# A hidden layer in two equal passes: one and a half chunks each instead of one and two

## The chip, the cores and the metric

The kernel runs on one core of a Trainium2 chip. The metric is the device time of one execution in microseconds, the median of the runs shown; the profile is of one further execution.

## The reference

`x` is 8 x 4224 x 192 in float32. First a causal convolution: each of 8 heads (24 channels) has 7 taps, normalized by a softmax. Then a feed-forward block with a residual, without biases:

```python
w = np.exp(w - max(w)); w = w / (sum(w) + 1e-09)
out = np.einsum('hk,bskhg->bshg', w, x_unf)       # x_unf: 7 shifted views of x
xn = (x - mu) / np.sqrt(var + 1e-06) * g_ln       # x is now out
ch = np.maximum(xn @ w_ch1, 0.0) @ w_ch2          # 192 -> 768 -> 192
return x + ch
```

## The kernel before

Tokens are worked off in 18 groups; a full group has 16 tokens in each of 128 partitions. The convolution of group g + 1 runs on VectorE (`conv`, six taps for each of 8 heads, one `scalar_tensor_tensor` each) while TensorE works on group g. The first two taps come from ScalarE (`first_tap`, `second_tap`) and are added by DMA on POOL's queue. VectorE also transposes y in 32 x 32 blocks to `yt`, so that channels lie on partitions in strips of 32.

Groups 3 to 17 are *mixed*: both matmuls are done as a 2 x 2 Strassen-Winograd product with seven products instead of eight. In the first matmul (`up_mixed`) the token halves and channel halves of `yt`, their sums (`ysums`), the quarters of the first weight and their sums (`w1sums`) enter; the quarters of the result are c11, c12, c21 and c22 of the hidden tile `room`. In float32 a matmul leaves two pairs of LDWEIGHTS and MATMUL records, and the four 32-row strips of TensorE run together.

A quarter has FC = 3 chunks of 128 hidden channels and 8 x 32 = 256 columns of tokens for each strip. PSUM has two sets of four banks of 512 columns, X and Y, one bank a strip. The seven products are therefore made in two passes: pass `one` with a single chunk (256 columns of a bank), then pass `two` with two chunks (512 columns). Products alternate between X and Y, so a product needs that the set of the product before the last was read. Each product is followed by one of:

- `evict`: ScalarE copies the set to a quarter (line L642);
- `close` with a part: ScalarE copies it to a part (L642), and a DMA on POOL's queue adds the part to a quarter (L609);
- `close` without one: VectorE adds the set to the quarter (L648).

Finished quarters get a relu in place on ScalarE (L655); c21 gets `lower_sum` on VectorE (L811), which also applies its relu and subtracts c11 for the second matmul. Then `down_fast` (L835) does the second matmul with seven products of its own on six banks, the first of which are those of X and Y; ScalarE copies them (L841), and between its products ScalarE does the rest of the relus, the scaling of the group before (L914) and the first taps of a later group.

There is no scheduler: each engine works off its instructions in the order of the program text, and an instruction that waits holds up those behind it on its engine. So the place of every call in `up_mixed` matters. In pass two the order around the change is: after the second product an eviction with its DMA; after the third and fourth an eviction each, with the relu of pass one's c11 (`one.relu(one.c11)`) behind the third; then on VectorE taps 2 to 4 of all heads and tap 5 of four heads (28 instructions, L417), the fifth product's close by DMA, the sixth product, the relu of pass two's c11, then on VectorE `lower_sum` of pass one, three more instructions of tap 5, and `close(c21)`; then the seventh product and its eviction.

`next(ahead)` stands for the last sums and transposes of the group before on VectorE (`finish_fast`), `next(pending)` for the halves of a reciprocal square root on POOL. `work` is the list of ScalarE's pieces that `down_fast` places between its products. In the last group the closes of pass two are on VectorE, `lower_sum` of pass one stands behind `close(c21)`, and four of the 16 tokens are left to a plain matmul at the end (`keep`, `down_row`).

Of the kernel before, what the change touches and what calls it, by code (L numbers as in the profile page):

```python
# [16 lines left out]
def kernel(  # L17
# [34 lines left out]
    P = 128  # L52
# [440 lines left out]
    def hidden_tile(g):  # L493
        n = groups[g][2]

        if fast[g]:
            ht[g] = room.rearrange(
                "p (h e f q j t) -> p h e f q j t", h=2, e=2, f=FC, q=NQ, t=width(g)
            )
        else:  # L500
            ht[g] = room[:, 0 : NF * NQ * n * C].rearrange(
                "p (f j q t) -> p f j q t", f=NF, q=NQ, t=C
            )
# [104 lines left out]
    def add_by_dma(dst, src):  # L608
        nc.gpsimd.dma_start(out=dst, in_=src, accum_op=ALU.add)  # L609

    def up_mixed(g, ahead, pending):


        W = HJ * C
        last = g + 1 == NG
        assert groups[g][2] == 2 * HJ and PAIR * W == 512 and FC == PAIR + 1
# [3 lines left out]
        s1, s2, s3, s4 = ysums[g]  # L620
        done = groups[g - 1][2]

        class Pass:
            def __init__(self, f0, f1, chain, other):
                self.n, self.chain, self.other = f1 - f0, chain, other
                self.b11, self.b12, self.b21, self.b22 = quarters_of_w1(f0, f1)
                self.t = [v[:, :, P * f0 : P * f1] for v in (w1sums[:, k] for k in range(3))]
                (self.c11, self.c12), (self.c21, self.c22) = [
                    [a[:, h, e, f0:f1].rearrange("p f q j t -> p f q (j t)") for e in range(2)]
                    for h in range(2)  # L630
                ]

            def product(self, to, left, right, first=True, end=True):
                rows_of_tiles(to, left, right, first, end, True)

            def seen(self, banks, f=None):
                src = banks[:, :, 0 : self.n * W] if f is None else banks[:, :, W * f : W * f + W]
                return src.rearrange("p q (f w) -> p f q w", w=W)

            def evict(self, banks, dst, relu=False, f=None):  # L640
                src = self.seen(banks, f)
                nc.scalar.activation(dst, src, AF.Relu) if relu else nc.scalar.copy(dst, src)  # L642

            def close(self, c, banks, part=None, f=None):


                if part is None:
                    nc.vector.tensor_tensor(c, c, self.seen(banks), op=ALU.add)  # L648
                    return
                self.evict(banks, part, f=f)  # L650
                whole = "p f q w -> p (f q w)"
                add_by_dma(c.rearrange(whole), part.rearrange(whole))

            def relu(self, c):
                nc.scalar.activation(c, c, AF.Relu)  # L655

        def parts(pool, tag):

            room = pool.tile([P, J * D], F32, tag=tag, name=f"parts_{tag}{g}")
            return room.rearrange("p (f q w) -> p f q w", q=NQ, w=W)  # L660

# [10 lines left out]
        one, two = Pass(PAIR, FC, X, Y), Pass(0, PAIR, Y, X)  # L672
        p = one
        p.product(X, a11, p.b11, True, False)
        p.evict(X, p.c11)
        p.product(Y, a12, p.b21)
        p.close(p.c11, Y, two.c12[:, 0:1])
        next(pending, None)
        p.product(X, s2, p.t[0], False, False)
        p.evict(X, p.c21)  # L680
        p.product(Y, s3, p.t[1], True, False)
        p.evict(Y, p.c22)
        p.product(X, s1, p.b12, False, False)
        p.close(p.c22, X, two.c12[:, 1:2])
        next(pending, None)
        p.product(Y, a22, p.t[2], False)
        p.close(p.c21, Y, two.c22[:, 0:1])
        p.product(X, s4, p.b22, False)
        p.evict(X, p.c12, True)

        next(ahead)
        p = two
        rooms = parts(cpool, "cs"), parts(bpool, "tb")
        p.product(Y, a11, p.b11, True, False)
        p.evict(Y, p.c11)
        p.product(X, a12, p.b21)
        if last:
            p.close(p.c11, X)
        else:
            for f in range(PAIR):  # L700
                p.close(p.c11[:, f : f + 1], X, rooms[0][:, f : f + 1], f)
            if g == 3:
                store_y(g, nc.gpsimd)
        act_scales(0, 1)
# [8 lines left out]
        p.product(Y, s2, p.t[0], False, False)  # L713
        p.evict(Y, p.c21)
        one.relu(one.c11)
        p.product(X, s3, p.t[1], True, False)
        p.evict(X, p.c22)
        act_scales(1, 2)
        p.product(Y, s1, p.b12, False, False)
        taps_of_next(2, 5)  # L720
        taps_of_next(5, 6, heads=(0, H // 2))
        p.close(p.c22, Y, None if last else rooms[1][:, 0:PAIR])
        p.product(X, a22, p.t[2], False)
        for f in range(PAIR):
            p.relu(p.c11[:, f : f + 1])
        if last:
            one.relu(one.c22)
        else:
            lower_sum(g, (PAIR,))
            taps_of_next(5, 6, heads=(H // 2, H - 1))  # L730
        p.close(p.c21, X)
        if last:
            lower_sum(g, (PAIR,))
        p.product(Y, s4, p.b22, False)
# [3 lines left out]
        lower_sum(g, range(PAIR))  # L738
        if last:

            n = J - fast[g]
            kept = xpool.tile([P, J + PAD, D], F32, tag="xg", name=f"kept{g}")
            kept = kept.rearrange("p j d -> p (j d)")[:, 0 : NF * n * P]
            kept = kept.rearrange("p (f j q h t) -> p f j q h t", f=NF, q=NQ, h=2, t=T)
            rows_left[g] = kept.rearrange("p f j q h t -> p f j (q h t)")

            def keep(f, h):
                src = a[:, h, f // FC, f % FC, :, fast[g] :].rearrange("p q j t -> p j q t")
                nc.scalar.activation(kept[:, f, :, :, h], src, AF.Relu)

            keeping = [lambda f=f, h=h: keep(f, h) for f in range(NF) for h in range(2)]
# [13 lines left out]
        work += [lambda j=j: scale_one(j) for j in range(2, done)]  # L765
        half = [lambda i=i: two.relu(two.c22[:, i : i + 1]) for i in range(PAIR)]
# [29 lines left out]
    def of_products(g):  # L796
        return ht[g][:, :, :, :, :, 0 : fast[g] * T // width(g), :]

    def half_sum(g, dst, left, right, op, fs=range(FC)):
        a = of_products(g)  # L800
        for f in fs:
            nc.vector.tensor_tensor(  # L802
                a[:, *dst, f], a[:, *left, f], a[:, *right, f], op=op
            )

    def lower_sum(g, fs=range(FC)):

        a = of_products(g)
        if g in MIXED:
            for f in fs:  # L810
                nc.vector.scalar_tensor_tensor(  # L811
                    out=a[:, 1, 0, f], in0=a[:, 1, 0, f], scalar=0.0, in1=a[:, 0, 0, f],
                    op0=ALU.max, op1=ALU.subtract,
                )
        else:
            half_sum(g, (1, 0), (1, 0), (0, 0), ALU.subtract, fs)

    def down_fast(g, work):
# [3 lines left out]
        a = of_products(g)  # L822
# [3 lines left out]
        free = a[:, 1, 0].rearrange("p f q j t -> p (f q) j t")  # L826
        parts = [free[:, 0:CH], free[:, CH : 2 * CH]]
        banks = [take_bank() for c in range(CH) for i in range(2)]

        def product(bank, left, right, to, first, behind=0):  # L830
            for c in range(CH):
                dst = banks[2 * c + bank]
                for f in (PAIR, *range(PAIR)):
                    for q in range(NQ):
                        nc.tensor.matmul(  # L835
                            dst[C * q : C * q + C, 0:w], right[:, f, C * c : C * c + C],
                            left[:, f, q], start=(first and f == PAIR), stop=(f == PAIR - 1),
                            skip_group_check=True,
                        )
                if to is not None:  # L840
                    nc.scalar.copy(  # L841
                        to[:, c], dst[:, 0:w].rearrange("p (j t) -> p j t", t=t)
                    )
                for one in work[:behind]:
                    one()
                del work[:behind]
# [15 lines left out]
        product(0, a[:, 0, 0], b[0], c11, True, behind[0])  # L862
        product(1, a[:, 1, 0], w2sums[:, 2], c22, True, behind[1])
        product(1, a[:, 1, 1], w2sums[:, 3], c21, False, behind[2])
        product(1, a[:, 0, 1], b[2], None, True, behind[3])
# [8 lines left out]
        for c in range(CH):  # L874
            nc.vector.tensor_tensor(
                c11[:, c], c11[:, c], banks[2 * c + 1][:, 0:w].rearrange("p (j t) -> p j t", t=t),
                op=ALU.add,
            )
        product(0, a[:, 1, 1], w2sums[:, 1], parts[0], False, 2)
        product(0, a[:, 0, 0], w2sums[:, 0], parts[1], False, 2)  # L880
        for one in work:
            one()
        product(0, a[:, 0, 1], b[3], c12, False)
# [207 lines left out]
```

## Time and profile before

| | |
|---|---|
| time, median of 3 runs | 956.37 us (956.06 to 957.61) |
| the profiled execution | 959.62 us |
| its span in the profile | 957.5 us |
| TensorE matmul busy | 950.6 us (99%) |
| VectorE busy | 890.7 us (93%) |
| ScalarE busy | 696.6 us (73%) |
| POOL busy | 338.4 us (35%) |
| L533, share of the chain that ended last | 47% |
| L835, share of the chain that ended last | 44% |
| one first matmul of a mixed group, 504 records | 27.96 us |
| one second matmul of a mixed group, 504 records | 27.44 us |

PE is TensorE's matmuls, PEld its weight loads, DVE VectorE, ACT ScalarE, POOL GpSimd. "In the records" means the start times of single instructions in the trace. The granted clock of TensorE was 1.00 in every stage looked at. The profiled execution's time is more than its span by what lies around the program.

### The profile page before, as it was taken

The page shows a single profiled execution, that of the slowest core. Times are in us where ns is not written, and L with a number is a line of the kernel's source. Part 1 is how long each engine was busy: PE and PEld are TensorE (multiplying, and loading weights), DVE is VectorE, ACT ScalarE, POOL GpSimd, SP SyncE. Part 2 cuts the span into 40 slices and gives each one's busy share as a digit, 9 for nine tenths or more (in the row PEclk, how much of TensorE's full clock was granted, in tenths as well). Part 3 has the DMA queues.
Part 4 walks back from the last instruction along what each step waited for, and adds up shares of the span by engine and source line. Part 5 has one row for each costly group of instructions (what it writes and reads, how often), then busy time and mean ns, then how long its engine had stood idle before and what let it go on. Part 6 is the DMA issues. An engine that isn't in the chain of part 4 may idle for free.

```text
span 957.5 us, 37878 instructions
## 1 busy us (share of the span) xinstructions
PE 950.6 (99%) x16858; PEld 743.1 (78%) x16858; DVE 890.7 (93%) x1489; ACT 696.6 (73%) x1165; POOL 338.4 (35%) x472
## 2 busy tenths in 40 slices
PE   9999999999999999999999999999999999999998
PEld 8998896876869697787968778695867769586787
DVE  7999999999999998999999999999999999999757
ACT  6853678596877959687795968779695877967462
POOL 1058422623145141533227141452316232261310
PEclk9999999999999999999999999999999999999999
DMA  8359589689697988979697896969889696778251
GB/s 204 101 160 212 98 230 280 121 187 229 135 263 138 249 156 181 224 132 277 127 249 151 196 220 127 278 131 252 155 197 205 124 276 132 175 136 138 42 96 68
DMA packets 39544, 168.82 MB, mean 176 GB/s; under 512 B 4437, under 2 KB 8150, under 8 KB 33367
## 3 DMA queue, kind: packets, MB, share of 16 engines
q0 software_dynamic: 32576, 106.25, 59.8%
q1 hardware_dynamic: 6800, 60.16, 17.3%
q8 instruction: 132, 2.16, 0.9%
q14 instruction: 30, 0.25, 0.1%
q10 hardware_dynamic: 6, 0.00, 0.0%
HBM read 38.93 MB, written 50.33 MB: 93 GB/s over the span
## 4 chain that ended last, share of the span: by engine, by line
PE 97%; POOL 1%; DMA 1%; ACT 0%; issue 0%; DVE 0%; ACTq 0%; POOLq 0%
PE ps L533 47%; PE ps L835 44%; PE ps L772 4%; PE ps L367 1%; DMA room<-room 1%; PE ps L326 1%; ACT room L642 0%; POOL room L609 0%; POOL d L460 0%; PE ps L354 0%; POOL r L483 0%; POOL d L479 0%; DVE yt L428 0%; POOL d L478 0%; PE ps L335 0%
## 5 line engine op out<-in xcount | busy, mean ns | idle before, releaser
L417 DVE SCALAR_TENSOR_TENSOR y<-xg,taps,y 128x384 f32<-128x384 f32 (+3 forms) x720 | 364.8, 583 | 1.9 <-DMA y<-room 1.3
L835 PE MATMUL ps<-room,w2sums 128*32 128x256 f32 (+2 forms) x4608 | 247.4, 371 | 0.0
L533 PE MATMUL ps<-yt,w 32*128 32x256 f32 (+2 forms) x4104 | 234.8, 378 | 0.3 <-DVE yt L428 0.3
L642 ACT COPY room<-ps 128x1024 f32<-128x1024 f32 (+1 forms) x135 | 175.0, 1296 | 78.6 <-PE ps L533 77.8
L533 PEld LDWEIGHTS ps<-yt,w 32*128 32x128 f32 x4104 | 204.1, 185 | 25.8 <-issue 8.7
L835 PEld LDWEIGHTS ps<-room,w2sums 128*32 128x32 f32 x4608 | 153.5, 110 | 87.8 <-ACT room L655 5.3
L835 PE MATMUL ps<-room,w 128*32 128x256 f32 (+2 forms) x3456 | 189.8, 371 | 0.1
L802 DVE TENSOR_TENSOR room<-room 128x1024 f32<-128x1024 f32 (+2 forms) x147 | 161.2, 1172 | 22.7 <-PE ps L835 16.1
L835 PEld LDWEIGHTS ps<-room,w 128*32 128x32 f32 x3456 | 113.9, 110 | 67.9 <-DVE room L648 5.0
L533 PE MATMUL ps<-ysums,w1sums 32*128 32x256 f32 x2160 | 125.3, 379 | 0.2 <-issue 0.2
L533 PEld LDWEIGHTS ps<-ysums,w1sums 32*128 32x128 f32 x2160 | 109.1, 185 | 11.2 <-ACT room L642 3.6
L925 POOL DMA_DIRECT2D out_dram<-ot x69 | 58.9, 940 | 159.3 <-ACT ot L914 102.6
L409 POOL DMA_DIRECT2D y<-tb x59 | 52.4, 1384 | 155.0 <-ACT room L841 110.2
L841 ACT COPY cs<-ps 128x256 f32<-128x256 f32 (+2 forms) x192 | 70.2, 367 | 45.6 <-PE ps L835 45.5
L655 ACT ACTIVATE room<-room 128x1024 f32<-128x1024 f32 (+1 forms) x89 | 92.5, 1072 | 0.8 <-DMA room<-parts_cs 0.8
L914 ACT ACTIVATE ot<-ot,r 128x192 f32<-128x192 f32 x224 | 90.9, 464 | 0.0
L380 ACT ACTIVATE y<-xg,taps 128x384 f32<-128x384 f32 (+3 forms) x141 | 73.1, 608 | 0.2 <-DMA xg<-in_x_dram 0.2
L448 DVE BATCH_NORM_STATS2 st<-y 128x6 f32<-128x192 f32 x264 | 70.1, 344 | 0.0
L841 ACT COPY room<-ps 128x256 f32<-128x256 f32 (+2 forms) x96 | 35.5, 369 | 46.5 <-PE ps L835 43.8
L398 ACT ACTIVATE tb<-xg,taps 128x384 f32<-128x384 f32 (+1 forms) x120 | 66.0, 627 | 0.0
L533 PE MATMUL ps<-yt,w1sums 32*128 32x256 f32 x1080 | 65.3, 380 | 0.4 <-ACT room L642 0.4
L533 PE MATMUL ps<-ysums,w 32*128 32x256 f32 x1080 | 64.6, 376 | 0.0
(113 smaller groups left out, 918.0 us busy)
## 6 DMA issues: line engine op xcount, KB each, us to landing
xg<-in_x_dram SPq DMA_DIRECT2D x14, 2112.0 KB, 16.6
room<-room POOLq DMA_DIRECT2D x45, 512.0 KB, 5.1
out_dram<-ot POOLq DMA_DIRECT2D x59, 384.0 KB, 9.6
y<-tb POOLq DMA_DIRECT2D x58, 384.0 KB, 8.5
out_dram<-y SPq DMA_DIRECT2D x13, 1536.0 KB, 9.5
room<-parts_cs POOLq DMA_DIRECT2D x28, 512.0 KB, 6.8
room<-parts_tb POOLq DMA_DIRECT2D x14, 1024.0 KB, 7.6
xg<-in_x_dram POOLq DMA_DIRECT2D x1, 2112.0 KB, 13.6
```

Source lines behind the costliest of these rows:

```text
L380: nc.scalar.mul(y[g][:, 0:n, cs], xg[g][:, 0:n, cs], taps[:, h, 0:1])
L398: nc.scalar.mul(tb[g][:, 0:n, cs], xg[g][:, 1 : 1 + n, cs], taps[:, h, 1:2])
L417: nc.vector.scalar_tensor_tensor(out=y[g][:, 0:n, cs], in0=t[:, k : k + n, cs], scalar=taps[:, h, k : k + 1], in1=y[g][:, 0:n, cs], op0=AL ...
L448: nc.vector.bn_stats(out=sums[g][:, j, :], in_=y[g][:, j, :])
L533: nc.tensor.matmul(banks[:, q, i * w : i * w + w], right[rows, c, P * i : P * i + P], left[rows, :, c, :], start=(first and c == 0 and i = ...
L642: nc.scalar.activation(dst, src, AF.Relu) if relu else nc.scalar.copy(dst, src)
L655: nc.scalar.activation(c, c, AF.Relu)
L802: nc.vector.tensor_tensor(a[:, *dst, f], a[:, *left, f], a[:, *right, f], op=op)
L835: nc.tensor.matmul(dst[C * q : C * q + C, 0:w], right[:, f, C * c : C * c + C], left[:, f, q], start=(first and f == PAIR), stop=(f == PAI ...
L841: nc.scalar.copy(to[:, c], dst[:, 0:w].rearrange("p (j t) -> p j t", t=t))
L914: nc.scalar.mul(ots[g][:, j, :], ots[g][:, j, :], rstd[g][:, j : j + 1])
L925: nc.gpsimd.dma_start(out=rows[:, d0:d1], in_=src[:, d0:d1], accum_op=ALU.add)
```

## The change

Both passes now have one and a half chunks: 256 columns of a whole chunk and 128 columns (half of the tokens) of the shared chunk 1, 384 columns of each bank. A product of a pass has, for each of 3 channel strips of 32 and each row strip, one matmul of 256 columns and one of 128, so 24 matmuls in each pass instead of 12 and 24. Evictions and closes all have 4 x 384 = 1536 elements a partition instead of 1024 or 2048. The hidden tile is laid out by pass; `down_fast` takes its chunks from it, and its column order within a bank changes for the last group.

The relu of pass one's c11 is cut into six pieces of 256 elements, one behind the eviction of each of six products: the last two of pass one and the first four of pass two. `lower_sum` and the sums of the second matmul take two instructions of 1536 elements instead of three of 1024. Pass one's c21 is closed by way of a part in the `cs` room instead of pass two's c22, so `next(ahead)` moves forward by two products; the second `next(pending)` moves behind that close. Of the two scalings in pass two one moves to behind the fifth product's close, the other to `work`. The close of pass two's c11 is one copy and one DMA instead of two of each. In the last group the copies of `keep` are 24 of 128 elements instead of 12 of 256.

```diff
-        if fast[g]:
+        if g in MIXED:
+            ht[g] = room.rearrange(
+                "p (h e r q s j t) -> p h e r q s j t", h=2, e=2, r=2, q=NQ, s=FC, t=width(g)
+            )
+        elif fast[g]:
...
-        W = HJ * C
+        W = HJ * C * FC // 2
+        M = 2 * HJ * C // PAIR
...
             def product(self, to, left, right, first=True, end=True):
-                rows_of_tiles(to, left, right, first, end, True)
+                pieces = [(of_tokens(left, None), PAIR * self.r, 0, M)]
+                pieces.append((of_tokens(left, self.r), 1, M, W))
+                for c in range(CH):
+                    for v, f, w0, w1 in pieces:
+                        for q in range(NQ):
+                            rows = slice(C * q, C * q + C)
+                            nc.tensor.matmul(
+                                to[:, q, w0:w1], right[rows, c, P * f : P * f + P],
+                                v[rows, ..., c, :], start=(first and c == 0 and w0 == 0),
+                                stop=(end and c == CH - 1), skip_group_check=True,
+                            )
...
-            def relu(self, c):
-                nc.scalar.activation(c, c, AF.Relu)
+            def relu(self, c, k=0, n=1):
+                c = c.rearrange("p q w -> p (q w)")
+                m = NQ * W // n
+                nc.scalar.activation(c[:, m * k : m * k + m], c[:, m * k : m * k + m], AF.Relu)
...
-        one, two = Pass(PAIR, FC, X, Y), Pass(0, PAIR, Y, X)
+        one, two = Pass(1), Pass(0)
+        low_one, low_two = [[part] for part in parts_of(g)]
...
-        p.close(p.c11, Y, two.c12[:, 0:1])
+        p.close(p.c11, Y, two.c12)
...
-        p.close(p.c22, X, two.c12[:, 1:2])
+        p.close(p.c22, X, two.c22)
+        next(ahead)
+        rooms = parts(cpool, "cs"), parts(bpool, "tb")
+        p.product(Y, a22, t[2], False)
+        p.close(p.c21, Y, rooms[0][:, 1])
         next(pending, None)
-        p.product(Y, a22, p.t[2], False)
-        p.close(p.c21, Y, two.c22[:, 0:1])
-        p.product(X, s4, p.b22, False)
+        one.relu(one.c11, 0, 6)
+        p.product(X, s4, b22, False)
         p.evict(X, p.c12, True)
-
-        next(ahead)
+        one.relu(one.c11, 1, 6)
+
         p = two
-        rooms = parts(cpool, "cs"), parts(bpool, "tb")
-        p.product(Y, a11, p.b11, True, False)
+        p.product(Y, a11, b11, True, False)
         p.evict(Y, p.c11)
-        p.product(X, a12, p.b21)
+        one.relu(one.c11, 2, 6)
+        p.product(X, a12, b21)
...
+        one.relu(one.c11, 3, 6)
...
         p.evict(Y, p.c21)
-        one.relu(one.c11)
+        one.relu(one.c11, 4, 6)
-        p.product(X, s3, p.t[1], True, False)
+        p.product(X, s3, t[1], True, False)
         p.evict(X, p.c22)
-        act_scales(1, 2)
+        one.relu(one.c11, 5, 6)
...
-        p.close(p.c22, Y, None if last else rooms[1][:, 0:PAIR])
-        p.product(X, a22, p.t[2], False)
-        for f in range(PAIR):
-            p.relu(p.c11[:, f : f + 1])
+        p.close(p.c22, Y, None if last else rooms[1][:, 0])
+        act_scales(0, 1)
+        p.product(X, a22, t[2], False)
+        for k in range(2):
+            two.relu(two.c11, k, 2)
         if last:
             one.relu(one.c22)
         else:
-            lower_sum(g, (PAIR,))
+            lower_sum(g, low_one)
             taps_of_next(5, 6, heads=(H // 2, H - 1))
         p.close(p.c21, X)
```

## The prediction

> **What bounds the kernel now.** First the page: busy times, and the chain that ended last by line.
>
> ```profile
> PE 950.6 (99%) x16858; PEld 743.1 (78%) x16858; DVE 890.7 (93%) x1489; ACT 696.6 (73%) x1165; POOL 338.4 (35%) x472
> PE 97%; POOL 1%; DMA 1%; ACT 0%; issue 0%; DVE 0%; ACTq 0%; POOLq 0%
> ```
>
> TensorE is the chain. The change touches the first matmul (L533) of the fifteen mixed groups; twelve of these stages last 27.96 us each. I take the one from 452.13 to 480.08, "the stage", and count times from 452.13. Its TensorE timeline (start, us, engine, line, count):
>
> ```profile
> 452.13 2.87 PE L533 MATMUL ps<-yt,w 32*128 32x256 f32 x48
> ...
> 460.38 6.83 PE L533 MATMUL ps<-yt,w 32*128 32x256 f32 x120
> 467.02 5.36 PE L533 MATMUL ps<-ysums,w1sums 32*128 32x256 f32 x96
> ...
> 477.38 2.77 PE L533 MATMUL ps<-yt,w 32*128 32x256 f32 x48
> 480.08 3.23 PE L835 MATMUL ps<-room,w 128*32 128x256 f32 x56
> ```
>
> A matmul leaves two records, and the four row strips run together, so four records make a row. The 96 records from 467.02 took until 472.20: 5.18/24 = 0.216 us a row. The stage has 126 rows, 27.20 us, and lasts 27.96. The missing 0.76 lies at product boundaries: the first seven products (6 rows, 1.30 each) should end at 9.07, yet in the records the second pass starts at 461.74, 0.54 late. ScalarE's timeline tells why:
>
> ```profile
> 453.77 1.01 ACT L642 COPY room<-ps 128x1024 f32<-128x1024 f32 x1 [1.16 <-PE ps L533]
> 455.06 1.01 ACT L642 COPY room<-ps 128x1024 f32<-128x1024 f32 x1 [0.28 <-PE ps L533]
> ...
> 469.86 1.87 ACT L642 COPY room<-ps 128x2048 f32<-128x2048 f32 x1 [0.31 <-PE ps L533]
> 471.62 1.06 ACT L655 ACTIVATE room<-room 128x1024 f32<-128x1024 f32 x1
> ```
>
> An eviction starts 0.25 after its product ended and takes 1.01; the product after next needs that bank set 1.30 after. 0.04 is left, and TensorE restarts late by 0.05 to 0.12.
>
> The end of the stage is VectorE's. Its timeline, then the waits inside the stage:
>
> ```profile
> 469.54 4.32 DVE L417 SCALAR_TENSOR_TENSOR y<-xg,taps,y 128x384 f32<-128x384 f32 x8
> 473.77 1.22 DVE L811 SCALAR_TENSOR_TENSOR room<-room 128x1024 f32<-128x1024 f32 x1
> 474.90 1.68 DVE L417 SCALAR_TENSOR_TENSOR y<-xg,taps,y 128x384 f32<-128x384 f32 x3
> 477.70 2.29 DVE L648 TENSOR_TENSOR room<-room,ps 128x2048 f32<-128x2048 f32 x1 [1.12 <-PE ps L533]
> 480.08 2.36 DVE L811 SCALAR_TENSOR_TENSOR room<-room 128x1024 f32<-128x1024 f32 x2
> ```
>
> ```profile
> DVE room L648 <- PE ps L533: 1.1, 1, 1.1
> PEld ps L835 <- DVE room L648: 0.3, 1, 0.3
> ```
>
> The down product takes the banks that `close(c21)` (L648) reads. That close ends at 479.99 and L835 starts at 480.08. So the stage ends on the chain lower_sum of pass one (L811), three convolutions (L417), close. There is 1.12 us of slack in it (0.86 in most of the other stages), before the close. The last row of the waits is that handover.
>
> **Matmuls.** Each product becomes 6 rows of 256 columns and 6 of 128, twice: 84 + 84 rows instead of 126. Streamed columns stay. Is a narrow row half a wide one? Two rows of the chain:
>
> ```profile
> 14.94 1.72 PE ps L326 x14
> ...
> 30.33 7.86 PE ps L533 x192
> ```
>
> 144 columns on the full array: 1.72/14 = 0.123 a record. 192 columns in strips: 7.86/48 = 0.164 a row. With 0.216 for 256 this is 0.833 ns a column plus 0.003, a weight load of 128 columns under each. Nearest is the warm-up matmul L367, 128 by 128: between 12.149 and 12.930 eight records start 0.1116 apart. Bounds 0.109 (the line) and 0.125 (the 144-column row, not beaten); I take 0.112. A product costs 6 x 0.216 + 6 x 0.112 = 1.97, fourteen 27.5: 0.3 above the 27.20 of before.
>
> The Trainium skill, "TensorE: Matmul & The Clock Gate", speaks against narrow rows: section "LDWEIGHTS (loading the stationary operand)" gives 128 columns / 1.2 = 107 ns per load, and section "The mechanism" lets a load overlap a running matmul "only when row_grp differs". By that a narrow row would cost some 107 + 107 ns, an estimate, and the change some 8 us a stage. L367 uses all strips and repeats every 0.112 with a load each, so the row decides.
>
> **Evictions.** 1536 elements lie between 1.01 (1024) and 1.87 (2048): 1.44. A set is free 0.25 + 1.44 = 1.69 after its product, needed at 1.97: 0.28 left instead of 0.04. The 0.5 us of boundary stalls goes (bounds 0.35 to 0.55). With a 256-element relu behind each eviction (L655: 1.06 for 1024 and 1.90 for 2048, so 0.43, of which 0.1 overlaps) a slot is 1.44 + 0.33 = 1.77 of 1.97; ScalarE keeps up. `act_scales(0,1)` (0.47) stands behind the fifth eviction of pass two instead and fits too.
>
> **The six relu pieces and what waits for them.** Before, the relu of pass one's c11 was one instruction after pass two's third product, done at 472.68 (20.55), and L811 came to it at 21.64 (21.4 to 22.3 in the other stages). Now the sixth piece stands behind the eviction of pass two's *fourth* product, the eleventh in all. That product ends at 0.10 + 11 x 1.97 = 21.8 (0.10: the late first row, as before). Eviction from 22.0 to 23.4, sixth piece to 23.75. lower_sum reads the whole of c11, so VectorE, ready at 21.6, stands about 2.1 us. Queued behind it, though not needing it, are the three convolutions and the close, and TensorE waits for the close:
> - lower_sum starts 23.85; 1536 elements is 1.22 + 512 x 1.04 ns = 1.76, the next starts 0.09 early: 25.5
> - three convolutions at 0.53: 27.1 (product thirteen ended at 25.7, so the close waits for nothing more)
> - close of 1536: 2.29 - 0.53 = 1.76, to 28.85; first L835 row at 28.95
>
> TensorE is through at 0.10 + 27.5 + 0.1 = 27.7, so it stands 1.2 us. The stage is 28.95 instead of 27.96: **+1.0**. The bounds: with 0.109 rows and no lag of lower_sum behind the piece 28.7 (+0.75), with 0.125 rows (2.05 a product) 29.8 (+1.85), halfway to these 29.3 (+1.35).
>
> **The down stage.** TensorE loses about 0.1 there at its third product, to a relu of c22 (L835 waits for L655, 5.3 us in 14 times, part of it in the load alone). ScalarE's work up to that relu is the same (one.c22 +0.43, two halves -0.43), but it now has 1.2 us more: -0.1. VectorE's sums in six of 1536 instead of nine of 1024 (1.67 against 1.13 each) save 0.2, and it waits there for TensorE anyhow: 0.
>
> **DMA adds.** 768 KB lands between the 512 KB row (median 5.1) and the 1024 KB row (7.6): 6.3. c11 of pass one is issued at 0.1 + 3.9 + 0.25 + 1.44 + 0.3 = 6.0, lands at 12.3; its first relu piece comes at 13.5. c21 is issued at 13.9 and lands by 22 even behind c22, before lower_sum. c11 of pass two is issued at 19.8, at 20.2 where the root's second half is ahead on POOL's queue, and lands near 26.5; its two relus end at 28.2, before L835 needs them at 29.3. Cover 1.2, 1.8 and 1.1 us. The first mixed group has slow adds (7.65 for 512 KB): there the first piece may wait 1.5, taken as +1.
>
> **Sum.** Fourteen stages at +1.0 - 0.1 = 12.6; the first +1 more; the stage at 729.66 lost 0.7 to a DMA add landing late on staging space that is now read earlier: -0.7. In the last group lower_sum stands behind the closes, so only the boundaries count: -0.5 + 0.3 = -0.2; twelve extra small copies there hide under a product without evictions. Together +12.7 us. The profiled execution took 959.62 with a span of 957.5, 3.3 above the median of 956.37. The difference goes on the median: **969**.
>
> **Rivals.** *The wait does not bind* (faster). If VectorE's stand behind the sixth piece is covered, the stage ends with TensorE at 27.7: -0.26, with -0.1 in the down stage -0.36 x 15 - 0.7 = -6: 950. It decides when the sixth piece ends before 22.5, since 5.2 us of queue follow it; for that the eleventh product would have to end at 20.5, 1.85 a product, below the narrowest row seen. Against it: the order of ScalarE's queue. For it: the boundary stalls are real.
> *Half of it*: the wait is only as long as the boundary gain, within 0.2% (about what a measurement tells): 956.
> *Narrow rows are bound by loads*: with the 0.185 us of a strip load (L533's LDWEIGHTS row) per narrow row a product is 2.41, a stage 33.9: +6 x 15 = 90, 1045. Against: L367.
> *Adds land late everywhere*: the first piece waits 1 us in every stage and delays TensorE and the chain: +14, 983. For: DMA is busy in the first 8 us of a stage; against: 1.2 us of cover.
>
> **How the numbers follow.** Vector wait 0.80 (its own range 964 to 974: +0.65 to +1.25 a stage over fourteen, the lower end without the first group's +1, the upper at rows halfway to 0.125, since L367 has the same width and the same load), not binding 0.08, half 0.05, loads 0.03, late adds 0.04. Slower by over 0.2%: 0.87; within: 0.05; faster: 0.08. The range reaches on both sides towards the next cases, 961 to 980: rows near 0.125, or late adds in part, above; a wait partly covered below.
>
> **What would show it.** Right: in ordinary stages L811's first lower_sum starts near 23.8 after an idle time given to ScalarE's relu; the close no longer waits for TensorE; TensorE stands about 1.2 us ahead of the down product; second pass starts at about 13.9; stage 28.9. Wrong: rows of 128 above 0.125, a stage below 28, or idle time at a DMA add.

## The result, and the profile after

The changed kernel takes 980.66 us (median of 4 runs, 979.98 to 982.59) against 956.99 for the kernel before beside it (4 runs): a ratio of 1.0246, 95% interval 1.0219 to 1.0272. It is slower by 23.7 us where 12.7 were forecast; 980.66 lies just above the range. The profiled execution took 980.75, with a span of 978.9. Of all runs below one, 986.52 us in the experiment with the close first, was slow for its kernel and is not counted.

First the page of the changed kernel: busy times, and two of the DMA queues (packets, MB, share of 16 engines' span).

```profile
PE 955.8 (98%) x19378; PEld 799.8 (82%) x19378; DVE 877.3 (90%) x1429; ACT 714.2 (73%) x1238; POOL 335.2 (34%) x458
...
q0 software_dynamic: 30560, 110.70, 59.9%
...
q8 instruction: 152, 2.49, 1.0%
```

TensorE has 2520 matmul records more, and as many loads. The last line is one that the prediction never looked at: a DMA queue that carries instructions, in packets of 16 KB. That they are TensorE's is read from the counts: 2 x 19378 matmuls and loads to 152 packets is 255 a packet; before it was 132 packets for 2 x 16858, again 255.

An ordinary stage is the one from 405.01 to 433.88. VectorE's timeline around its end (start, us, engine, line; in brackets the idle time before it and its releaser). L856 is the lower sum, L417 the convolutions, L666 the close:

```profile
423.46 3.78 DVE L417 SCALAR_TENSOR_TENSOR y<-xg,taps,y 128x384 f32<-128x384 f32 x7
428.81 1.76 DVE L856 SCALAR_TENSOR_TENSOR room<-room 128x1536 f32<-128x1536 f32 x1 [1.57 <-ACT room L675]
430.49 1.67 DVE L417 SCALAR_TENSOR_TENSOR y<-xg,taps,y 128x384 f32<-128x384 f32 x3
432.08 1.75 DVE L666 TENSOR_TENSOR room<-room,ps 128x1536 f32<-128x1536 f32 x1
```

The lower sum starts 23.80 into the stage after idle time given to ScalarE's relu, and the close no longer waits for TensorE: it stands directly behind the convolutions and ends 28.82 us into the stage. ScalarE's timeline shows the piece that VectorE stood for, the L675 at 428.36, behind the eviction (L661) of the eleventh product:

```profile
427.02 1.44 ACT L661 COPY room<-ps 128x1536 f32<-128x1536 f32 x1 [0.26 <-ACT room L675]
428.36 0.42 ACT L675 ACTIVATE room<-room 128x256 f32<-128x256 f32 x1
```

The waits of the whole run (engine, line, waited for: us in total, times, longest). L887 is the down product, L653 the up product:

```profile
DVE room L856 <- ACT room L675: 30.4, 15, 4.9
PEld ps L887 <- DVE room L666: 14.7, 14, 1.2
PEld ps L653 <- issue: 14.4, 30, 1.2
PE ps L887 <- DVE room L666: 12.0, 14, 1.1
PE ps L653 <- issue: 4.2, 9, 1.0
```

The second and fourth rows are one wait, once in each of fourteen stages, seen by weight load and matmul: TensorE stands about 1.1 us for the close in ten of them, and less in four that have a stop late in the stage. The third and fifth are something else. "issue" is idle time for which no semaphore is to blame. In the third row, 15 of the 30 times (6.0 us) are a wait at the start of each up stage, which before has too; the others, and the fifth row, fall inside products. In the kernel before, two rows tell of stops of the same kind:

```profile
PE ps L533 <- issue: 0.2, 1, 0.2
PEld ps L835 <- issue: 1.2, 3, 0.6
```

In after, TensorE's timeline of the stage from 347.42 (30.01 us long) and of the first mixed stage (from 118.53, 31.94 us) shows where:

```profile
365.62 1.48 PE L653 MATMUL ps<-ysums,w1sums 32*128 32x256 f32 x30
367.51 3.00 PE L653 MATMUL ps<-ysums,w1sums 32*128 32x128 f32 x66 [0.40 <-issue]
...
377.44 0.42 PE L887 MATMUL ps<-room,w 128*32 128x256 f32 x4 [1.03 <-DVE room L666]
```

```profile
122.42 1.59 PE L653 MATMUL ps<-yt,w 32*128 32x256 f32 x32 [0.99 <-issue]
...
133.95 4.96 PE L653 MATMUL ps<-yt,w 32*128 32x128 f32 x114 [0.78 <-issue]
```

Set beside the packets of queue q8 in the same records, each of these stops ends 1.2 to 1.5 us after a packet has landed. In the stage from 347.42:

```
packet 351.92 to 352.86   (16 and more other DMA transfers ran at once until about 351.5)
packet 359.35 to 360.32   (until about 358.7)      TensorE resumes 361.59, 0.28 lost
packet 365.33 to 366.31   (amid DMA adds)          TensorE resumes 367.51, 0.56 lost
```

The places of the stops settle what they are. Count TensorE's instructions in the records, its semaphore waits included: from the first mixed stage on, and leaving out the waits at the starts of up stages, all 15 stops of at least 0.26 us in after lie whole multiples of 256 instructions apart. So do all 119 such stops in the thirteen traces of this document. 256 instructions are one packet: TensorE stops at the end of one block of 256 because the next has not arrived.

Such a block is 32 rows of four strips. In rows of 256 columns that is 32 x 0.216 = 6.9 us of work; in the mixed rows, half of them of 128 columns, 16 x 0.327 = 5.2 us. A packet takes 0.95 us, and no stop ended less than 1.2 us after the landing. So, as an estimate, a packet may start 5.2 - 0.95 - 1.2 = 3.1 us after TensorE began the block before it, and 4.8 us in rows of 256 columns. The second and third packets above started 3.4 and 3.7 us after it.

By stages, the span's +21.4 us is, to 0.2: fourteen up stages at 28.87 instead of 27.96, +12.7; stops in stages two to fourteen (347.42, 461.44, 574.74, 744.68, 858.79 above all), +4.6; the first mixed stage, beyond its 0.91, +2.65; the last group, up 28.94 instead of 28.29 and down 21.47 instead of 20.76, +1.4; the down stages, 27.57 instead of 27.44 in most, +0.6 in sum; the long stage at 729.66 of before, -0.7.

### The profile page after: what moved, and what is told of

Read it like the earlier page. It is cut to its first block, busy times and chain, and to the rows that moved or that the text cites. A ratio compares the mean times of both kernels' runs of the same rounds, so it can differ in the third digit from the quotient of the medians.

```text
span 978.9 us, 42818 instructions
## 1 busy us (share of the span) xinstructions
PE 955.8 (98%) x19378; PEld 799.8 (82%) x19378; DVE 877.3 (90%) x1429; ACT 714.2 (73%) x1238; POOL 335.2 (34%) x458
## 5 line engine op out<-in xcount | busy, mean ns | idle before, releaser
L417 DVE SCALAR_TENSOR_TENSOR y<-xg,taps,y 128x384 f32<-128x384 f32 (+3 forms) x720 | 364.9, 581 | 1.9 <-DMA y<-room 1.5
L887 PE MATMUL ps<-room,w2sums 128*32 128x256 f32 (+2 forms) x4608 | 252.3, 371 | 0.0
L661 ACT COPY room<-ps 128x1536 f32<-128x1536 f32 x120 | 172.7, 1439 | 77.8 <-PE ps L653 73.1
L887 PEld LDWEIGHTS ps<-room,w2sums 128*32 128x32 f32 x4608 | 170.5, 110 | 72.2 <-issue 0.3
L887 PE MATMUL ps<-room,w 128*32 128x256 f32 (+2 forms) x3456 | 196.3, 371 | 12.4 <-DVE room L666 12.0
L653 PE MATMUL ps<-yt,w 32*128 32x256 f32 (+1 forms) x4320 | 191.0, 324 | 2.2 <-issue 2.1
L653 PEld LDWEIGHTS ps<-yt,w 32*128 32x128 f32 x4320 | 181.7, 186 | 11.9 <-issue 9.7
L849 DVE TENSOR_TENSOR room<-room 128x1536 f32<-128x1536 f32 (+2 forms) x99 | 155.8, 1642 | 39.1 <-PE ps L887 39.1
L887 PEld LDWEIGHTS ps<-room,w 128*32 128x32 f32 x3456 | 126.2, 110 | 69.2 <-DVE room L666 14.7
L653 PE MATMUL ps<-ysums,w1sums 32*128 32x128 f32 (+1 forms) x2880 | 126.7, 323 | 1.9 <-issue 1.9
L653 PEld LDWEIGHTS ps<-ysums,w1sums 32*128 32x128 f32 x2880 | 120.4, 186 | 5.6 <-issue 3.4
L675 ACT ACTIVATE room<-room 128x256 f32<-128x256 f32 (+2 forms) x164 | 107.0, 672 | 11.4 <-DMA room<-parts_cs 11.2
L856 DVE SCALAR_TENSOR_TENSOR room<-room 128x1536 f32<-128x1536 f32 (+1 forms) x30 | 51.9, 1731 | 31.6 <-ACT room L675 30.4
L653 PE MATMUL ps<-ysums,w 32*128 32x128 f32 (+1 forms) x1440 | 67.0, 323 | 0.3 <-issue 0.2
L653 PE MATMUL ps<-yt,w1sums 32*128 32x256 f32 (+1 forms) x1440 | 66.7, 323 | 0.0
```

The costliest lines, as they stand in the source:

```text
L417: nc.vector.scalar_tensor_tensor(out=y[g][:, 0:n, cs], in0=t[:, k : k + n, cs], scalar=taps[:, h, k : k + 1], in1=y[g][:, 0:n, cs], op0=AL ...
L653: nc.tensor.matmul(to[:, q, w0:w1], right[rows, c, P * f : P * f + P], v[rows, ..., c, :], start=(first and c == 0 and w0 == 0), stop=(end ...
L675: nc.scalar.activation(c[:, m * k : m * k + m], c[:, m * k : m * k + m], AF.Relu)
L849: nc.vector.tensor_tensor(part(*dst), part(*left), part(*right), op=op)
L887: nc.tensor.matmul(dst[C * q : C * q + C, 0:w], right[:, f, C * c : C * c + C], rows_of_chunk(g, *left, f, q), start=(first and f == PAIR) ...
```

## The experiments

Two theories stood at the start. *A*: the sixth relu piece, with VectorE's queue behind it, sets the end of the stage. *F*: TensorE waits for its own instructions, which get through late because of the DMA adds. The rival to both is that TensorE's narrower rows are simply dear. Times are medians, each beside runs of the kernel before on the same chip (956.99 to 957.62). "After" in the diffs is the changed kernel.

**Close first.** After, with the close and its convolutions ahead of the lower sum:

```
-        else:
-            lower_sum(g, low_one)
-            taps_of_next(5, 6, heads=(H // 2, H - 1))
+        taps_of_next(5, 6, heads=(H // 2, H - 1))
         p.close(p.c21, X)
-        if last:
-            lower_sum(g, low_one)
+        lower_sum(g, low_one)
```

> The changed kernel (980.66 us) with one thing moved: in the fourteen groups that are not the last, VectorE's close of c21 and the three convolutions behind it are put ahead of pass one's lower sum, which needs the late relu pieces. Theory A (VectorE's queue behind the sixth relu piece sets the end of the stage): the close starts when the thirteenth product has ended, near 26.0 into the stage, the up stage is 27.8 instead of 28.87, TensorE no longer stands 1.1 us ahead of the down product, and the whole is 14 x 1.05 = 15 us shorter: 966 (964 to 968). Rival B (TensorE's own rows and stops fill the stage, and the wait for the close only shows them): 979 to 982. Rival C (the lower sum, now later, holds up the second product of the down stage instead, wanted 3.9 us after its start): 970 to 978, with idle time ahead of that product.

Measured: 975.25 us (971.89 to 979.02), ratio 1.0186 (1.0163 to 1.0210). VectorE's timeline of the same place (stage from 176.23):

```profile
202.20 1.76 DVE L666 TENSOR_TENSOR room<-room,ps 128x1536 f32<-128x1536 f32 x1 [2.16 <-PE ps L653]
203.87 3.42 DVE L853 SCALAR_TENSOR_TENSOR room<-room 128x1536 f32<-128x1536 f32 x2
```

The close waits for TensorE again, starts 25.97 into the stage, and the stage is 27.78: A's mechanism to the tenth. But only 5.4 of its 15 us come out. The other up stages last up to 29.20 with stops (7.2 us in stages two to fourteen, 4.6 in after), and the fourteen down stages sum to 396.4 us instead of 386.0, 7.3 of it in one stage where ScalarE stood 5.6 us for a DMA add. TensorE's waits do not name the lower sum, so it is not rival C. The wait was real, but it had been covering stops.

**Relu in four pieces.** After, with pieces only in the first four places, of four:

```
-        one.relu(one.c11, 0, 6)     # and 1, 2, 3 likewise
+        one.relu(one.c11, 0, 4)
...
-        one.relu(one.c11, 4, 6)
-        one.relu(one.c11, 5, 6)
```

> The changed kernel with the relu of pass one's c11 in four pieces of 384 elements in the first four of the six places, so that it is done near 20.1 into the stage instead of 23.77; VectorE's order is as in the changed kernel. Theory A (the place of the last piece in ScalarE's queue is the cause): the lower sum starts at 21.6 to 22.3 with no idle time, the close waits for the thirteenth product, stage 27.8, 966 (964 to 968), the same as with the close ahead. Rival B (six pieces or four, the cost is that of smaller instructions on ScalarE, or of TensorE's rows): 978 to 982. If an eviction with a 384-element piece behind it (1.44 + 0.45 = 1.89 of a product's 1.97) no longer fits, stalls at product boundaries would take back up to 0.3 us a stage: 970.

Measured: 971.89 us, 1.0149 (1.0130 to 1.0168): 8.8 of A's 15 us. VectorE's timeline (stage from 175.60) and its waits for the lower sum in the whole run:

```profile
198.80 1.76 DVE L854 SCALAR_TENSOR_TENSOR room<-room 128x1536 f32<-128x1536 f32 x1 [0.96 <-DMA room<-parts_cs]
```

```profile
DVE room L854 <- DMA room<-parts_cs: 9.7, 9, 2.3
DVE room L854 <- ACT room L675: 4.1, 10, 1.1
```

With the relu done at 20, the lower sum still starts at 23.2 in this stage: now it waits for c21's DMA add. In after this add lands at about 23.0, some 0.7 us before the sixth piece ends, so that this second wait was hidden by the first. Up stages are 28.1 to 29.4, with stops in some as before.

**The late relu alone.** The kernel before, with its relu of c11 in six pieces in the changed kernel's places:

```
-        one.relu(one.c11)
+        one.relu(one.c11, 4, 6)     # 0 to 3 in the places before it
         p.product(X, s3, p.t[1], True, False)
         p.evict(X, p.c22)
+        one.relu(one.c11, 5, 6)
```

> The kernel before (956.99 us) with only the second part of the change: the relu of pass one's c11 in six pieces of 170 or 171 elements in the places of the changed kernel, the last behind the eviction of pass two's fourth product; the passes stay one chunk and two. Theory A (the late relu costs only because the lower sum it holds up and the work behind it are longer, and the slack of 0.86 to 1.12 us ahead of the close takes it here): last piece at 22.4, lower sum 0.1 to 0.8 us later than before, stage 27.96 to 28.1, 957 (956 to 960; up to 2 of this from two pieces that follow evictions of 1.01 us in slots of 1.30). Rival B (the late relu is by itself the whole cost): 968 to 971.

Measured: 957.97 us, 1.0005 (0.9996 to 1.0014). VectorE's timeline (stage from 451.42; L819 the lower sum, L648 the close):

```profile
473.93 1.23 DVE L819 SCALAR_TENSOR_TENSOR room<-room 128x1024 f32<-128x1024 f32 x1 [0.52 <-ACT room L658]
...
476.92 2.29 DVE L648 TENSOR_TENSOR room<-room,ps 128x2048 f32<-128x2048 f32 x1 [0.18 <-PE ps L533]
```

The lower sum waits 0.52 us, and the close still has 0.18 of slack. The same late relu costs nothing where the lower sum is 1024 wide and the last relu piece ends at 22.5. It took the equal passes to make it cost.

**The narrow rows alone.** The kernel before, with the second chunk of each pass-two product in two rows of 128 columns, 168 rows a stage:

```
-                rows_of_tiles(to, left, right, first, end, True)
+                pieces = [(left, 0, 0, W)]
+                pieces += [
+                    (left[:, n * r : n * r + n], 1, W + h * r, W + h * r + h) for r in range(2)
+                ]
...
```

> The kernel before with only more, narrower rows: in pass two the second chunk of each product in two rows of 128 columns instead of one of 256, so that a stage has 168 rows instead of 126, as many instructions as the changed kernel; passes, evictions, relus and VectorE as before. Row cost alone: 84 rows of 0.111 to 0.112 for 42 of 0.216 is +0.25 to 0.35 a stage, 15 stages, +4 to +5: 961 to 962 (rival R). Theory F (the changed kernel's stops in the middle of products are TensorE waiting for its instructions, which come in packets of 16 KB, 256 instructions, behind the DMA adds): the same stops, without a semaphore, show up in the records here, some 4 to 9 us in all, and the whole is 965 to 971. Rival L (the load of 128 columns is not hidden): over 1000.

Measured: 983.97 us, 1.0272 (1.0248 to 1.0296): +26.5, more than the whole change, and far above F's 965 to 971. TensorE's timeline of its longest up stage (from 631.51, 30.93 us; L646 is the product in mixed rows), and the waits of its weight loads (L851 the down product):

```profile
646.50 5.50 PE L646 MATMUL ps<-ysums,w1sums 32*128 32x256 f32 x129
652.56 0.61 PE L646 MATMUL ps<-ysums,w1sums 32*128 32x128 f32 x12 [0.56 <-issue]
...
658.50 1.27 PE L646 MATMUL ps<-yt,w1sums 32*128 32x128 f32 x28 [1.05 <-issue]
```

```profile
PEld ps L646 <- issue: 10.0, 12, 2.1
PEld ps L851 <- issue: 9.9, 10, 1.8
```

Four up stages last exactly 28.27, 0.31 more than before: that is the price of the rows. The rest are stops: 10.3 us in up stages two to fourteen, 2.5 in the first, 7.6 in the down stages. They are there with relus, evictions and VectorE as before. A load that is not hidden is out: it would be in every stage.

**No adds.** After, without the DMA adds of its closes:

```
                 self.evict(banks, part)
-                add_by_dma(*[v.rearrange("p q w -> p (q w)") for v in (c, part)])
```

> The changed kernel without the DMA adds of its closes (five of 768 KB in a mixed group, three in the last): the parts are still evicted to their staging rooms, but are never added, so this part of the sum is left out of the result. The DMA adds of the second tap and of the output stay. Theory F (TensorE's stops without a semaphore in the middle of products are packets of its own instructions, which start only at the end of a DMA add): the stops of the up stages go, the stages that lasted 29.3 to 31.9 come down to 28.87, where the sixth relu piece still holds them, and the whole is 980.7 - 8.5 = 972 (970 to 975). Rival R (168 rows a stage are too many instructions for the packets however free the DMA is): the stops stay, 979 to 982.

Measured: 976.24 us, 1.0199 (1.0183 to 1.0216); the profiled execution took 974.75. From its page, as many instruction packets beside half the bytes of the adds' queue, and the waits of the weight loads:

```profile
q0 software_dynamic: 20048, 53.29, 30.2%
...
q8 instruction: 151, 2.47, 1.0%
```

```profile
PEld ps L886 <- DVE room L666: 17.6, 14, 1.3
PEld ps L653 <- issue: 8.3, 17, 1.2
```

In the last row, 15 of the 17 times are the wait at the start of the up stage; the other two are in the first mixed stage. Eleven of stages two to fourteen are 28.88 to 28.90, the longest 29.06: 0.3 us of stops in all, where after has 4.6. One down stage has a stop, of 0.7. The wait for the close is untouched. The last group comes down to 28.26 and 20.61. The first mixed stage keeps its stops (31.39): there the DMA engines carry other traffic (a 16-engine load from 119 to 125.5). F holds in stages two to fourteen; but the median is 1.2 above the range that F gave, and the gain is 4.4 us where 8.5 were forecast, in part because the first mixed stage keeps its stops.

**Adds in halves.** After, each add as two of 384 KB:

```
-                add_by_dma(*[v.rearrange("p q w -> p (q w)") for v in (c, part)])
+                for k in range(2):
+                    add_by_dma(*[
+                        v.rearrange("p q w -> p (q w)")[:, 2 * W * k : 2 * W * k + 2 * W]
+                        for v in (c, part)
+                    ])
```

> The changed kernel with each DMA add of its closes issued as two of 384 KB, one behind the other on the same queue; same bytes. Theory S (an instruction packet is let in between two adds, and waits for the end of the one that runs): the packets wait half as long, the stops fall from 8.5 us to about 3 to 5, the whole is 975 to 978. Rival N (a packet waits for all that is queued, or the adds' issue on GpSimd becomes the limit): 980 to 985.

Measured: 978.32 us, 1.0217 (1.0199 to 1.0234); this overlaps the changed kernel's interval. Stops in the up stages fall from 7.7 to 4.7 us, but a down stage got one of 1.35. The total decides nothing. The records speak against S: in up stages two to fourteen the median packet starts 1.54 us after TensorE began the block before it, in after 1.55, and not half of that.

**The relu of c22 cut by width.** After:

```
-        half = [lambda k=k: two.relu(two.c22, k, 2) for k in range(2)]
+        def relu_of_width(w0, w1):
+            v = two.c22[:, :, w0:w1]
+            nc.scalar.activation(v, v, AF.Relu)
+
+        half = [lambda w0=w0, w1=w1: relu_of_width(w0, w1) for w0, w1 in ((0, M), (M, W))]
```

> The changed kernel with one thing in the down stage: the relu of pass two's c22 in two pieces along the width (256 of each strip's 384 columns, then 128) instead of two strips and then the other two. Theory W (the down stages last 27.57 instead of the forecast 27.35 because two strips of the third product are released by the first relu half and the other two, 0.2 us later, by the second, and the strips stay out of step to the end): in the records the four strips of a row start together again, down 27.40 (27.36 to 27.45), -0.15 x 14 = -2: 978.5 (the stops of the up stages may shift this by 2 either way, so the stage in the records decides). Rival (another cause): 27.57 as before it.

Measured: 979.94 us, 1.0245 (1.0224 to 1.0265), and down stages of 27.33 in twelve of fourteen. Starts of matmuls in the third down product, from the records, in us from the start of the down stage (from 319.85 in after, from 317.94 by width):

```
after     8.226 8.233 | 8.442 8.449   two strips a row ahead, to the end
by width  8.226 8.233   8.239 8.246   four together, to the end
```

W is shown. In after, half a relu covers two strips, these run a row ahead, and the stage is a row longer at its end. Of the 0.24 x 14 = 3.4 us gained, the total shows 0.7, which is within the noise: the profiled execution had more stops (7.9 us in stages two to fourteen).

**Both causes away.** After, with the edits of the no-adds run and of the four pieces together:

```
-                add_by_dma(*[v.rearrange("p q w -> p (q w)") for v in (c, part)])
...
-        one.relu(one.c11, 0, 6)     # and 1, 2, 3 likewise
+        one.relu(one.c11, 0, 4)
...
-        one.relu(one.c11, 4, 6)
-        one.relu(one.c11, 5, 6)
```

> Both causes taken away: the changed kernel without the DMA adds of its closes (this part of the sum is left out of the result) and with the relu of pass one's c11 in four pieces, the last done near 20. If the late relu (with the DMA add of c21 behind it) and the instruction packets behind the adds are all there is: up stages 27.8 throughout, whole 980.7 - 8.5 - 14 x 1.07 = 957 (955 to 959). If the narrow rows cost more than 0.112, or something third holds the stages, 962 or more.

Measured: 961.56 us, 1.0043 (1.0027 to 1.0059). Up stages are 27.78 in ten of stages two to fourteen, the others up to 28.23. VectorE's timeline (stage from 234.94):

```profile
257.07 1.75 DVE L853 SCALAR_TENSOR_TENSOR room<-room 128x1536 f32<-128x1536 f32 x1
...
260.92 1.75 DVE L666 TENSOR_TENSOR room<-room,ps 128x1536 f32<-128x1536 f32 x1 [0.51 <-PE ps L653]
```

No wait for relu or add, and 0.51 of slack ahead of the close. What is left above the forecast of 957 is the first mixed stage: its stops remain, and it lasts 33.61, 5.8 more than the others. The four pieces gain 8.8 us, the missing adds 4.4, both together 19.1, 5.9 more than the sum. Two things lie in that, and no run parts them: c21's add, which holds up the lower sum in the run of the four pieces, goes with the adds; and the two causes cover each other. The second can be seen in after: the stages from 234.48 and 688.24 lose 0.26 and 0.36 us to stops late in the stage and still last 28.87, because TensorE then stands 0.6 and 0.7 us less for the close.

**Narrow rows without adds, and the control.** The two kernels that carry no change but the rows, and no change at all, each without the adds. To the kernel of the narrow rows, and to the kernel before:

```
                 self.evict(banks, part, f=f)
-                whole = "p f q w -> p (f q w)"
-                add_by_dma(c.rearrange(whole), part.rearrange(whole))
```

> The kernel before with only the narrow rows in pass two (983.97 us with the DMA adds of its closes) and without those adds: the parts are evicted and never added, so this part of the sum is left out of the result. Relus, evictions and VectorE as before. Theory F (the 27 us that the narrow rows cost alone are their instruction packets starting late, at the ends of DMA adds, and only 0.3 us a stage is the rows): up stages 28.27 throughout apart from the first, 957 + 15 x 0.31 = 962 (960 to 965, since the first group also has loads in its way). Rival R (168 rows a stage need more packets than can be had in time on a quiet DMA too): over 975.

> Control: the kernel before without the DMA adds of its closes (this part of the sum is left out of the result). Theory F (126 rows of 256 columns a stage leave the packets, one in 6.9 us, time to wait for an add): hardly anything to gain, stages 27.96 as they are, only the stage that had a DMA add land late (28.65) and the first come down: 955 to 957. Rival (the adds delay TensorE or the evictions in any kernel that has them, by a common factor): the same 4 us or more that the changed kernel gained, or the 20 us that the narrow rows alone should gain: 935 to 953.

Measured: 963.53 us, 1.0061 (1.0043 to 1.0079), and 956.91 us, 0.9999 (0.9988 to 1.0010). In the first all thirteen stages two to fourteen last 28.27, and the waits for instructions in the mixed rows have shrunk to this:

```profile
PEld ps L646 <- issue: 0.4, 1, 0.4
```

So in stages two to fourteen the stops need both, as F has it: the adds cost the kernel before nothing, and the kernel with narrow rows 20 us. 168 rows without adds fit, 126 rows beside adds fit but for a few small stops, 168 rows beside adds do not. The first mixed stage, where loads run, keeps stops in both kernels (29.28 and 29.36 us).

**All mends together.** After, with the edits of the close first, the four pieces, the adds in halves and the cut by width; the whole sum is computed:

```
+        taps_of_next(5, 6, heads=(H // 2, H - 1))
         p.close(p.c21, X)
+        lower_sum(g, low_one)
...
+        one.relu(one.c11, 0, 4)     # and 1, 2, 3; no 4 and 5
...
+                for k in range(2):  # add_by_dma on half k
...
+        half = [lambda w0=w0, w1=w1: relu_of_width(w0, w1) for w0, w1 in ((0, M), (M, W))]
```

> The changed kernel with the four mends together: four relu pieces, the close and its convolutions ahead of pass one's lower sum, adds in halves, c22's relu cut by width. All of the sum is computed. The two VectorE waits (sixth piece, and c21's DMA add behind it) are gone, so up stages that have no late packet last 27.8 and down stages 27.33. What is left is the packets: with some 8 to 15 us of stops, now that TensorE stands for nothing else, 953 + 8 to 15 = 961 to 968. If halves let packets through well enough for stops under 4 us, it would match the kernel before: 957. If the close ahead makes the down stage wait for the lower sum or for c22, as in part of the stages with the close alone, 970.

Measured: 968.07 us, 1.0115 (1.0093 to 1.0136), the upper end of what was forecast. Clean stages are 27.78 and 27.33, together 0.29 shorter than before's, but stops take 7.3 us in up stages two to fourteen and 4.0 in the down stages:

```profile
PEld ps L653 <- issue: 13.1, 24, 1.3
PEld ps L890 <- issue: 3.0, 3, 1.7
```

No version with 168 rows beat the kernel before; the most that its clean stages could give is 0.29 x 14 = 4 us.

## Why the prediction was right and wrong

**Right: sign, mechanism and main term.** The sixth piece ends at 23.77 (forecast 23.75), the lower sum starts at 23.80 (23.85), the close is through at 28.82 (28.85), the stage lasts 28.87 (28.95). TensorE stands 1.1 us (1.2). Fourteen times +0.91 is 12.7 where the sum had 14.0. The experiments add that a second wait, c21's DMA add, stood close behind: its landing was forecast "by 22" and came at about 23.0.

**Right: the rows.** 256 and 128 columns together take 0.327 us (0.216 + 0.112 forecast), and the narrow rows alone 0.31 a stage. The Trainium skill's rule that the prediction weighed ("TensorE: Matmul & The Clock Gate", section "The mechanism": a load overlaps a running matmul "only when row_grp differs") would have given some 8 us a stage by the prediction's estimate; the measured 0.31 decides against such a cost here.

**Wrong: what the extra rows cost beside their columns.** The step "84 + 84 rows instead of 126. Streamed columns stay" priced a row by its columns and never its instructions. So a block of 256 instructions was never set against the packet that must bring the next, and the term stood at nothing without a reason. The trace of before would have shown it: the queue (132 instruction packets), and three stops of the same kind at ends of blocks, at 122.63, 332.74 and 725.64, 1.4 to 1.6 us after a packet landed. The term measured +4.6 us in stages two to fourteen. The same cause is in the two terms that were mis-sized: the first mixed stage, where "+1 more" for late adds was +2.65, and the last group, where -0.2 was +1.4, 0.9 of it stops in the records. The range's upper end had been drawn from rows near 0.125 and from late adds; the rows came at 0.111, and in most stages no add was late enough to hold the relu pieces.

**Wrong: the down stage.** "-0.1 each" is what the run with the cut by width shows, 27.33 us instead of before's 27.44; but the new cut of c22's relu, costed at nothing, put the strips out of step and took 0.24 at the end. In sum +0.6 us instead of -1.4; it is not more because three down stages of before's profiled execution were 0.3 to 0.5 us longer than the rest.

**The base.** Of the 11.7 us between 969 and 980.66, the terms above are 8.5: stops +4.6, down stages +2.0, first +1.65, last +1.6, main term -1.3. The other 3.2 are that the difference was put on a median 3.3 below before's profiled execution, while after's profiled execution lies at its median.

**The rivals.** "Adds land late everywhere" gave 983, near the time, but not by its mechanism: the first relu piece starts at 13.47 in most stages, as forecast. The adds do cost time, through TensorE's instructions. "Narrow rows are bound by loads" and "the wait does not bind" are refuted, the latter by the close-first run's stages.

**How late the packets are.** From the records of up stages two to fourteen, the time from TensorE's start on a block to the start of the next block's packet: in after the median is 1.55 us, and 14 of 68 packets come later than the 3.1 us that mixed rows leave; without the adds the median is 0.06, and none of 70 comes so late. In the kernel before the median is 1.3 with adds and below zero without, and the latest, 4.8, just reaches what rows of 256 columns leave. So the adds delay packets in both kernels, and the narrow rows turn the delay into stops. Open: by what rule a packet is held back beside an add.

## What to carry to other kernels

Splitting a matmul costs instructions as well as columns: count TensorE's instruction packets in the DMA queues, and compare the work that a packet holds (5.2 us here instead of 6.9) with how late packets come beside other DMA traffic (up to 4.4 us in after's up stages). Two stands of an engine in one stage can cover each other, so mend them together before saying what either is worth. Where a producer is cut in pieces, cut it so that all strips of its consumer are released together.

## What the runs showed of the hardware

- TensorE's instructions arrive by DMA in 16 KB packets of 256; a packet takes 0.95 us, and a starved TensorE resumes 1.2 to 1.6 us after it has landed. All 119 stops of at least 0.26 us without a semaphore lie at ends of blocks of 256 instructions. Beside DMA adds a packet starts later (median 1.55 us instead of 0.06 after the block before). With 126 rows a stage this cost nothing (956.91 without adds, 957.05 with); with 168 it cost 20 us (963.53 and 983.97).
- Rows of 128 columns in strips of 32 rows, each with its own weight load, repeat every 0.111 us.
- Column strips that start out of step stayed so: 0.2 us between two pairs at the third down product was still there 19 us later.
